# Fused attention and Fourier mixing: three copies of turned u on another engine, and some steps in another order

## The chip, the cores and the metric

The kernel runs on one core of a Trainium2 chip. The metric is the device time of the whole kernel in microseconds (us), the median of several runs. The engines are TensorE (PE, with its weight loads as PEld), VectorE (DVE), ScalarE (ACT) and GpSimd (POOL). SyncE (SP) does nothing but issue transfers (DMA); GpSimd and ScalarE issue a few as well.

## The reference

There are 8 batches of 8 heads, with 512 rows `x` and 32 rows `state` of 64 numbers for each head. Cut to what matters:

```
scores = scale * x @ state.T         # 512 x 32 for each head
xread  = softmax(scores)  @ state    # 512 rows
sread  = softmax(scale * state @ x.T) @ x   # 32 rows
x = concat(xread, sread)             # (8, 544, 512), heads side by side
u = x + real(fft(fft(x, axis=1), axis=2))
un = (u - mean(u)) / sqrt(var(u) + 1e-6)
out = u + relu(un @ w_ch1) @ w_ch2   # 512 -> 2048 -> 512
```

## The kernel before

The Fourier transforms are products with tables of sines and cosines. The 544 rows of a batch are folded onto each other, so that one product gives a row and its mirrored row. A batch passes through these stages:

- **Reading (`attend`).** The input rows lie in `xin` as bf16 with the rows on the partitions. For the scores they must be turned: `xT`, and `sT` for the state. Batches 0 and 1 turn on TensorE; from batch 2 on SyncE issues DMA transposes (L377 and L388, four for `xT`). `scores(i)` does 8 matmuls (L422) into one PSUM buffer, `esp`, and ScalarE takes the exponential into `E` (L427). The first call needs the first two of four row blocks, the second the other two. `turn_scores(g)` turns `E` by TensorE (L434), and ScalarE copies the result to `ET` (L435). The reads are then matmuls with `ET` (L447), divided by their sums on VectorE (L455, L456); the per head read of the state rows (`sread_by_head`, L467) ends in five VectorE operations (L470, L474). Folds on VectorE (L516 to L536) and GpSimd (L501 to L513) follow.
- **Mixing (`transform`).** `over_s` (L774) is the transform over rows, `over_d` (L670, L671) over columns. VectorE adds them to the reads, which gives four tiles `U[k, r]` of 128 rows. Each has its mean and variance taken on VectorE (L337, L339); GpSimd works out the root (L343, L344); and the centred tile `ub` is written by ScalarE (L814, L831) or VectorE (L812, L833). `turn_u(k, r)` turns it into a quarter of `unT`: on TensorE with a copy out of PSUM (L842, L843) in batches 0 and 1, by a DMA transpose (L838) from batch 2 on. In a later batch `centre(k, r)` does statistics and centring in one step.
- **The layers.** `layer1` has 16 steps (L917, or L927 in quarters for batch 0) that need `unT` and end in a Relu on ScalarE (L919, L929). `layer2` has four quarters for each of four tiles (L982), and the last quarter ends in `store`: VectorE scales and adds (L949), SyncE writes. Mirrored tiles go over `r_dram` (L963), and their second transfer (L964) is issued at the next store. The 32 state rows of a batch are kept for later in `XLs` by a ScalarE copy, `keep_middle` (L857), which `done1` calls for batch 1.

[...] the order of calls is the schedule. For batches 0 and 1 it is written out call by call (L1111 to L1244). There `L` and `M` are the steps of layer 1 and 2 of batch 0, `s1` and `r1` the scores and reads of batch 1, `turn_u` and `centre_sums` those of batch 0, and `turn_u1`, `centre1` and `done1` those of batch 1. In the loop at b = 1, `M1`, `L1`, `R`, `T` are layer 2 of batch 0 (from M[7] on), layer 1 of batch 1, the reads of batch 2 and the mixing of batch 2; `s2` and `s3` are the scores of batches 2 and 3. `T[7]` turns (0, 1) and centres (1, 1), `T[8]` turns (0, 0) and centres (1, 0), `M1[8]` is M[15], the last store of batch 0. From b = 2 on `weave` mixes the streams: each stream has a start and an end between 0 and 1, step i of n is put at start + (end − start)(i + 0.5)/n, and the steps are sorted. At b = 3 the reads are those of batch 4, and layer 2 is batch 2's.

PSUM is shared out in pools: `psQ` has three buffers that turned tiles, scores, turned scores and both transforms take in turn; `psF` has three for both layers; `psX` has one for the reads. A buffer is taken again once the last operation that reads it is done.

Of the kernel before, what the change touches and what calls it, by code (L numbers as in the profile page):

```python
# [30 lines left out]
def kernel(  # L31
# [8 lines left out]
    nc = tc.nc  # L40
# [71 lines left out]
    def load_state(lo, hi, src=state):  # L112
        nc.sync.dma_start(
            out=states(lo, hi).rearrange("p b g d -> p (b g) d"),
            in_=src[lo:hi].rearrange("b (g hh) j d -> (hh j) (b g) d", hh=4),
        )
# [4 lines left out]
    def load_x(b):  # L121
        xs = xs_of[b] if b in xs_of else wk.tile([128, 4 * dm], F32, name="xs", tag="xs")
        xs_of[b] = xs
        v = xs.rearrange("p (i h d) -> p i h d", i=4, d=D)
        xb = x[b].rearrange("h s d -> s h d")
        row = v[15:32:16, 3]
        parts = [
            (v[:, 0], xb[1:129]),
            (v[:, 1], xb[144:272]),
            (v[:, 2], xb[273:401]),  # L130
            (v[32:128, 3], xb[416:512]),
            (v[0:15, 3], xb[129:144]),
            (v[16:31, 3], xb[401:416]),
            (row, xb[0:273:272]),
        ]
        if b == 0:
            for queue, n in ((nc.sync, None), (nc.scalar, 2), (nc.sync, 3), (nc.scalar, 0), (nc.sync, 4), (nc.sync, 5), (nc.sync, 6),
                             (nc.sync, 1)):
                if n is None:
                    load_state(0, 1)  # L140
                else:
                    queue.dma_start(out=parts[n][0], in_=parts[n][1])
            return
        for o, rows in parts:
            nc.sync.dma_start(out=o, in_=rows)

    def cast_x(b, copy=nc.gpsimd.tensor_copy, lo=0, hi=4):
        copy(xin_bufs[b % 2][:, lo:hi, 1:513], xs_of[b].rearrange("p (i c) -> p i c", i=4)[:, lo:hi])  # L148
# [16 lines left out]
    def state_blocks(lo, hi, copy=nc.scalar.copy):  # L165
        for hh in range(4):
            pq = slice(32 * hh, 32 * hh + 32)
            copy(stb[pq, lo:hi, :, 4 + 64 * hh:68 + 64 * hh], states(lo, hi)[pq])
# [189 lines left out]
    turned = {}  # L358
# [546 lines left out]
    def layer1(key):  # L905
        low = isinstance(key, tuple)
        n = 128 if low else 512
        hT = wk.tile([128, FC, n], BF16, name="hTL" if low else "hT", tag="hTL" if low else "hT", bufs=1 if low else 2)
        h_of[key] = hT
        per = 512 // n  # L910

        def step(i):
            ph = psF.tile([128, 512], F32, name="ph", tag="c")
            for f in range(per * i, per * i + per):
                o = (f % per) * n
                for c in range(DC):
                    nc.tensor.matmul(ph[:, o:o + n], lhsT=w1[:, c, f * 128:(f + 1) * 128], rhs=un_of[key][:, c, :],  # L917
                                     start=(c == 0), stop=(c == DC - 1))
            nc.scalar.activation(hT[:, per * i:per * i + per, :].rearrange("p a b -> p (a b)"), ph, AF.Relu,  # L919
                                 scale=-1.0 / 512 if key == 0 else -1.0 if key in flipped else 1.0)  # L920

        def quarter_step(i, r):
            ph = psF.tile([128, 512], F32, name="ph", tag="c")
            for f in range(4 * i, 4 * i + 4):
                o = 128 * (f % 4)
                for c in range(DC):
                    nc.tensor.matmul(ph[:, o:o + 128], lhsT=w1[:, c, f * 128:(f + 1) * 128],  # L927
                                     rhs=un_of[key][:, c, 128 * r:128 * r + 128], start=(c == 0), stop=(c == DC - 1))
            nc.scalar.activation(hT[:, 4 * i:4 * i + 4, 128 * r:128 * r + 128], ph.rearrange("p (a b) -> p a b", b=128),  # L929
                                 AF.Relu, scale=-1.0 / 512 if key == 0 else -1.0 if key in flipped else 1.0)  # L930

        if key == 0:
            return [lambda i=i, r=r: quarter_step(i, r) for r in range(4) for i in range(FC // 4)]
        return [lambda i=i: step(i) for i in range(FC // per)]
# [55 lines left out]
    def weave(*streams):  # L990
        todo = []
        for n, (steps, lo, hi) in enumerate(streams):
            for i, s in enumerate(steps):
                if s is not None:
                    todo.append((lo + (hi - lo) * (i + 0.5) / len(steps), n, i, s))
        for _, _, _, s in sorted(todo, key=lambda t: t[:3]):
            s()
# [19 lines left out]
    begin, terms_of, low_of, out_of, keep_low, over_d, add_sums, centre_sums, turn_u, spread, done, keep_middle = transform(0)  # L1017
# [85 lines left out]
    s1, r1 = attend(1)  # L1103
    scores_next, reads_after = attend(2)
    L, M = layer1(0), layer2(0)
    over_s1, over_d1, add1, centre1, turn_u1, done1 = transform(1)
    turns1, copies1, s1 = s1[0], s1[1:4], s1[4:]
# [29 lines left out]
    L[1]()  # L1137
    turn_u(0, 0)
    s1[0]()
    s1[1]()  # L1140
    add_sums(1, 1)
    add_sums(1, 0)
    L[2]()
    L[3]()
    s1[2]()
    s1[3]()
# [10 lines left out]
    r1[4]()  # L1157
    r1[3]()
    centre_sums(1, 0)
    turn_u(1, 1)  # L1160
    L[7]()
    r1[5]()
    L[8]()
# [43 lines left out]
    centre1(1, 0)  # L1207
    done()
    first_roots[0]()
    M[3]()  # L1210
    spread(0, 0)
    first_roots[5]()
    M[7]()
    turn_u1(1, 1)
    M[8]()
    turn_u1(1, 0)
    done1()
    l2, scores_first = M, scores_next
    for b in range(1, B + 1):
        reads_next = reads_after  # L1220
        l2, l2_now = (layer2(b), [l2[7]] + l2[8:]) if b == 1 else (layer2(b) if b < B else [], l2)
        early, until, start = {2: (7, 0.25, 0.22), 3: (3, 0.13, 0.1)}.get(b, (0, 0, 0.08))
        l2_now = l2_now + (layer2(("L", b // 4)) if b in (3, 7) else [])
        streams = [(l2_now[:early], 0, until), (l2_now[early:], until + 0.02 if early else 0, 1)]
        if b == 1:
            M1, L1, R, T, s2 = l2_now, layer1(1), reads_next, transform(2), scores_first
            scores_next, reads_after = attend(3)
            s3 = scores_next
            def spreads():
                spread(1, 1)  # L1230
                spread(1, 0)
                for root in first_roots[6:8]:
                    root()

            def roots():
                for root in first_roots[1:5]:
                    root()

            for step in (spreads, M1[2], s2[0], s2[1], L1[0], M1[3], s2[2], s2[3], L1[1], lambda: cast_x(3), turned[3], L1[2],
                         lambda: load_state(4, B, s_dram), lambda: load_x(4), R[0], L1[3], R[1], roots, M1[4], R[2], L1[4], R[3], L1[5], R[4],  # L1240
                         L1[6], M1[5], R[6], L1[7], R[7], L1[8], M1[6], R[8], L1[9], L1[10], M1[7], T[0], T[1], L1[11], T[2], T[3],
                         L1[12], T[4], L1[13], s3[0], T[5], L1[14], s3[1], T[6], L1[15], T[7], M1[8], T[8], s3[2], s3[3], T[9], T[10],
                         T[11], lambda: state_blocks(4, B, nc.gpsimd.tensor_copy)):
                step()  # L1244
            continue
        if b < B:
            streams.append((layer1(b), start, 1))
        if b + 1 < B:
            reads, mix = {2: ((0.1, 0.45), (0.57, 0.88)), 3: ((0.03, 0.4), (0.5, 0.86))}.get(b, ((0, 0.375), (0.47, 0.85)))
            streams.append((reads_next, *reads))  # L1250
            streams.append((transform(b + 1), *mix))
        if b + 2 < B:
            scores_next, reads_after = attend(b + 2)
            streams.append(([lambda: (cast_x(b + 2), turned[b + 2]())], 0.2, 0.2))
            streams.append((scores_next, 0.5, 1))
        if b + 3 < B:
            streams.append(([lambda: load_x(b + 3)], 0.35, 0.35))
        if b in (3, 7):
            streams.append((low_rows(b // 4), 0.02, 0.2))
            streams.append((layer1(("L", b // 4)), 0.36, 0.8))  # L1260
        weave(*streams)
# [30 lines left out]
```

The softmax here doesn't subtract the row's maximum and nothing guards it: scores larger than these inputs give would overflow.

## Time and profile before

| what | value |
|---|---|
| time, median of 3 | 300.76 us (300.56 to 300.85) |
| span of the profiled run | 298.8 us |
| TensorE busy | 285.7 us, 96% |
| VectorE busy | 176.6 us, 59% |
| ScalarE busy | 139.5 us, 47% |
| GpSimd busy | 91.8 us, 31% |
| a matmul of 512 columns in either layer | 379 ns from start to end, 0.216 us from start to start |
| copy of turned u out of PSUM (L843) | 417 ns on VectorE (5 of them), 567 ns on ScalarE (3 of them) |

"Busy" is the time in which an engine has work, a share of the span. A row of the timeline gives a group's start and length in us, its engine, its line in the kernel, the operation with the tiles that it writes and reads, the shape, how many there are, and in brackets the engine's idle time before it with what ended that. Starts are counted from the first instruction. A few matmul records are missing, so a group of 3 may be one of 4.

### The profile page before, as it was taken

What the parts mean: (1) busy time and instruction counts of PE and PEld (TensorE: products, weight loads), DVE (VectorE), ACT (ScalarE), POOL (GpSimd) and SP (SyncE); (2) the same over time, 40 slices, a digit from 0 to 9 for tenths busy, and PEclk for the clock granted to TensorE, in tenths of its full rate; (3) what the DMA queues carried; (4) which work ended last, traced back from release to release, by engine and by line L of the source; (5) the groups of instructions that cost most, each with busy time, mean ns of one, the idle gap of its engine ahead of it and who ended that gap; (6) DMA issues with size and microseconds to landing.
All of it is one profiled execution on the core that took longest, in us unless ns stands there. A gap on an engine that the chain in (4) does not pass through costs nothing.

```text
span 298.8 us, 6004 instructions
## 1 busy us (share of the span) xinstructions
PE 285.7 (96%) x2288; PEld 163.3 (55%) x2319; DVE 176.6 (59%) x441; ACT 139.5 (47%) x260; POOL 91.8 (31%) x227
## 2 busy tenths in 40 slices
PE   5999899899899999999999999999999999999995
PEld 4689785445445544566444554455444544555443
DVE  8865789576769488645548394757567574111122
ACT  6888575545824662354523543344524443334200
POOL 6764833393590045202242033402240121000000
PEclk9999999999999999999999999999999999999999
DMA  9999993956965932684343955153332034400345
GB/s 157 189 203 198 149 169 63 172 140 144 192 132 101 225 69 58 136 161 119 81 105 80 187 104 142 38 116 78 99 96 43 30 89 98 113 24 16 98 117 135
DMA packets 110824, 34.86 MB, mean 117 GB/s; under 512 B 101980, under 2 KB 106332, under 8 KB 110796
## 3 DMA queue, kind: packets, MB, share of 16 engines
q1 hardware_dynamic: 100076, 28.72, 44.6%
q0 software_dynamic: 4224, 4.19, 9.7%
q10 hardware_dynamic: 6496, 1.57, 2.6%
q8 instruction: 18, 0.29, 0.5%
q14 instruction: 10, 0.08, 0.1%
HBM read 22.41 MB, written 14.02 MB: 122 GB/s over the span
## 4 chain that ended last, share of the span: by engine, by line
PE 82%; DVE 12%; ACT 2%; issue 2%; POOL 1%; DVEq 0%; POOLq 0%; ACTq 0%
PE po L982 33%; PE ph L917 32%; PE ph L927 5%; PE gp L774 3%; DVE st L337 2%; DVE U L675 2%; PE yp L670 1%; PE yp L671 1%; PE po L974 1%; DVE ot L949 1%; PE xrp L447 1%; PE eTp L434 1%; PE esp L422 1%; PE gp L717 1%; PE xfp L447 1%
## 5 line engine op out<-in xcount | busy, mean ns | idle before, releaser
L982 PE MATMUL po<-w,hT 128*128 128x512 bf16 x482 | 121.3, 379 | 1.2 <-issue 0.5
L919 ACT ACTIVATE hT<-ph 128x512 bf16<-128x512 f32 x112 | 66.9, 597 | 111.2 <-PE ph L917 109.7
L917 PE MATMUL ph<-unT,w 128*128 128x512 bf16 x431 | 111.8, 379 | 1.0 <-DVE ot L949 0.3
L917 PEld LDWEIGHTS <-w 128*128 128x128 bf16 x576 | 50.4, 98 | 46.1 <-issue 0.9
L982 PEld LDWEIGHTS <-hT 128*128 128x128 bf16 x496 | 46.8, 98 | 47.5
L949 DVE SCALAR_TENSOR_TENSOR ot<-po,rstd,U 128x512 f32<-128x512 f32 (+2 forms) x33 | 24.1, 731 | 51.7 <-PE po L982 46.0
L778 POOL COPY GL<-G 128x128 bf16<-128x128 bf16 x7 | 2.0, 291 | 68.3 <-ACT G L775 68.3
L337 DVE BATCH_NORM_STATS2 st<-U 128x6 f32<-128x512 f32 x32 | 21.8, 682 | 0.1
L344 POOL TENSOR_TENSOR rstd<-rstd,mhalf 128x1 f32<-128x1 f32 x34 | 20.8, 611 | 2.7
L343 POOL TENSOR_TENSOR rstd<-mv,epst 128x1 f32<-128x1 f32 x34 | 6.7, 198 | 47.2 <-DVE mv L339 47.2
L675 DVE TENSOR_TENSOR U<-yp,XR 128x512 f32<-128x512 f32 x14 | 9.5, 680 | 19.7 <-PE yp L671 19.7
L927 PE MATMUL ph<-unT,w 128*128 128x128 bf16 x256 | 15.6, 219 | 1.1 <-DVE unT L843 1.1
L927 PEld LDWEIGHTS <-w 128*128 128x128 bf16 x256 | 14.7, 98 | 1.5 <-DVE unT L843 1.1
L775 ACT CAST G<-gp 128x288 bf16<-128x288 f32 x28 | 12.9, 482 | 4.9 <-PE gp L774 4.9
L148 POOL CAST xin<-xs 128x2048 bf16<-128x2048 f32 (+1 forms) x9 | 11.7, 1319 | 2.6 <-DMA xs<-in_x_dram 2.5
L929 ACT ACTIVATE hT<-ph 128x512 bf16<-128x512 f32 x16 | 9.5, 599 | 5.7 <-PE ph L927 5.6
L455 DVE RECIPROCAL rs<-xrp 128x8 f32<-128x8 f32 x14 | 2.9, 206 | 14.2 <-PE xrp L447 14.2
L833 DVE TENSOR_SCALAR ub<-U,mv 128x512 bf16<-128x512 f32 x20 | 10.3, 514 | 0.7
L501 POOL COPY XT<-XR 32x514 bf16<-32x514 bf16 x7 | 4.2, 603 | 21.0 <-DVE XR L456 19.9
L456 DVE TENSOR_TENSOR XR<-xrp,rs 128x512 bf16<-128x512 f32 x14 | 9.7, 694 | 0.5
L456 DVE TENSOR_TENSOR XF<-xfp,rs 128x512 bf16<-128x512 f32 x14 | 9.7, 691 | 0.5
L427 ACT ACTIVATE E<-esp 128x512 bf16<-128x512 f32 x14 | 8.3, 596 | 3.1 <-PE esp L422 3.0
(240 smaller groups left out, 377.8 us busy)
## 6 DMA issues: line engine op xcount, KB each, us to landing
xs<-in_x_dram SPq DMA_DIRECT2D x22, 256.0 KB, 4.6
w<-in_moe_w_ch_dram POOLq DMA_DIRECT2D x8, 512.0 KB, 10.2
out_dram<-ot SPq DMA_DIRECT2D x15, 256.0 KB, 3.7
r_dram<-ot SPq DMA_DIRECT2D x14, 256.0 KB, 2.2
out_dram<-r_dram SPq DMA_DIRECT2D x14, 256.0 KB, 3.6
xs<-in_x_dram SPq DMA_DIRECT2D x8, 192.0 KB, 4.7
xs<-in_x_dram ACTq DMA_DIRECT2D x2, 256.0 KB
l_dram<-ot SPq DMA_DIRECT2D x2, 256.0 KB
```

Source lines behind the costliest of these rows:

```text
L148: copy(xin_bufs[b % 2][:, lo:hi, 1:513], xs_of[b].rearrange("p (i c) -> p i c", i=4)[:, lo:hi])
L337: nc.vector.bn_stats(st6, u)
L344: nc.gpsimd.tensor_tensor(rstd, rstd, mhalf, op=ALU.pow)
L456: nc.vector.tensor_tensor(ov, in0=p[ps, :, 0:256].rearrange("p g (h d) -> p g h d", d=D), in1=rs[ps].unsqueeze(3).to_broadcast([n, 2, 4, D ...
L675: nc.vector.tensor_add(u.rearrange("p (k r) -> p k r", r=2), p.rearrange("p (r k) -> p k r", r=2)[:, 0:u.shape[1] // 2, :], x.rearrange("p ...
L775: nc.scalar.copy(G[:, j, :].rearrange("p (i q) -> p q i", q=2), p[:, 0:NM].rearrange("p (q i) -> p q i", q=2))
L833: nc.vector.tensor_scalar(t, in0=ud, scalar1=mv[:, 0:1], scalar2=None, op0=ALU.subtract)
L917: nc.tensor.matmul(ph[:, o:o + n], lhsT=w1[:, c, f * 128:(f + 1) * 128], rhs=un_of[key][:, c, :], start=(c == 0), stop=(c == DC - 1))
L919: nc.scalar.activation(hT[:, per * i:per * i + per, :].rearrange("p a b -> p (a b)"), ph, AF.Relu, scale=-1.0 / 512 if key == 0 else -1.0 ...
L927: nc.tensor.matmul(ph[:, o:o + 128], lhsT=w1[:, c, f * 128:(f + 1) * 128], rhs=un_of[key][:, c, 128 * r:128 * r + 128], start=(c == 0), st ...
L949: nc.vector.scalar_tensor_tensor(ot[:, cols], in0=po_of[i][:, 0:cols.stop - cols.start], scalar=rstd, in1=u[:, cols], op0=ALU.mult, op1=AL ...
L982: nc.tensor.matmul(po_of[i], lhsT=h_of[key][:, f, i * 128:(i + 1) * 128], rhs=w2[:, f, :], start=(f == 0), stop=(f == FC - 1))
```

## The change

The change touches the order and one choice of engine; no computation is added or taken away.

- Three copies of turned u, batch 0's (1, 1) and batch 1's (1, 1) and (1, 0), go from VectorE to ScalarE. VectorE's queue is then clear of them.
- The second scores of batch 1 (`s1[1]`) come after the step `L[2]` and batch 0's additions rather than right after the first scores, so that they don't wait for a buffer of `psQ`.
- `M[3]`, which ends in a store, comes after the statistics of batch 0's (0, 0) and its root.
- `done1` moves from before the loop to behind the turned scores of batch 2.
- In the loop at b = 1, `T[7]` and `T[8]`, which centre batch 2's tiles on ScalarE, move behind the turned scores of batch 3 (`s3[2]`, `s3[3]`); `M1[8]` is then ahead of both.
- At b = 3 the reads begin at 0.04 instead of 0.03. By the rule of `weave` this changes one place: the per head read of batch 4 goes from 0.174 to 0.18, behind layer 2's store at 0.175.

```diff
     s1[0]()
-    s1[1]()
     add_sums(1, 1)
     add_sums(1, 0)
     L[2]()
+    s1[1]()
     L[3]()
...
     centre_sums(1, 0)
-    turn_u(1, 1)
+    turn_u(1, 1, nc.scalar.copy)
     L[7]()
...
     first_roots[0]()
-    M[3]()
     spread(0, 0)
     first_roots[5]()
+    M[3]()
     M[7]()
-    turn_u1(1, 1)
+    turn_u1(1, 1, nc.scalar.copy)
     M[8]()
-    turn_u1(1, 0)
-    done1()
+    turn_u1(1, 0, nc.scalar.copy)
...
-            for step in (spreads, M1[2], s2[0], s2[1], L1[0], M1[3], s2[2], s2[3], L1[1], lambda: cast_x(3), turned[3], L1[2],
+            for step in (spreads, M1[2], s2[0], s2[1], L1[0], M1[3], s2[2], s2[3], done1, L1[1], lambda: cast_x(3), turned[3], L1[2],
...
-                         L1[12], T[4], L1[13], s3[0], T[5], L1[14], s3[1], T[6], L1[15], T[7], M1[8], T[8], s3[2], s3[3], T[9], T[10],
+                         L1[12], T[4], L1[13], s3[0], T[5], L1[14], s3[1], T[6], L1[15], M1[8], s3[2], s3[3], T[7], T[8], T[9], T[10],
...
-            reads, mix = {2: ((0.1, 0.45), (0.57, 0.88)), 3: ((0.03, 0.4), (0.5, 0.86))}.get(b, ((0, 0.375), (0.47, 0.85)))
+            reads, mix = {2: ((0.1, 0.45), (0.57, 0.88)), 3: ((0.04, 0.4), (0.5, 0.86))}.get(b, ((0, 0.375), (0.47, 0.85)))
```

## The prediction

> **What bounds the kernel now.** I read the page's busy line first, then the waits of TensorE, then TensorE's timeline for where they lie, then the same microseconds on ScalarE, GpSimd and SyncE.
>
> ```profile
> PE 285.7 (96%) x2288; PEld 163.3 (55%) x2319; DVE 176.6 (59%) x441; ACT 139.5 (47%) x260; POOL 91.8 (31%) x227
> ```
>
> TensorE is busy for 96% of the span, and the change takes no matmul away. All it can win is TensorE's idle time. In the timeline the bracket is the idle time before a group and what ended it:
>
> ```profile
> 24.95 0.39 PE L422 MATMUL esp<-sT,xT 128*128 128x64 bf16 x8 [0.21 <-DVE unT L843]
> 33.38 1.07 PE L927 MATMUL ph<-unT,w 128*128 128x128 bf16 x16 [0.78 <-DVE unT L843]
> ...
> 54.17 0.39 PE L422 MATMUL esp<-sT,xT 128*128 128x64 bf16 x8 [0.84 <-DVE unT L843]
> ...
> 78.25 2.75 PE L982 MATMUL po<-w,hT 128*128 128x512 bf16 x12
> 81.80 0.28 PE L447 MATMUL xrp<-stb,ET 128*128 128x260 bf16 x1 [0.79 <-ACT ET L435]
> 82.37 0.28 PE L447 MATMUL xrp<-stb,ET 128*128 128x260 bf16 x1 [0.29 <-ACT ET L435]
> ...
> 86.62 1.04 PE L917 MATMUL ph<-unT,w 128*128 128x512 bf16 x3
> ...
> 119.66 1.02 PE L917 MATMUL ph<-unT,w 128*128 128x512 bf16 x4 [0.29 <-DVE ot L949]
> ```
>
> The bracket is a little short of the loss: a run of 12 matmuls takes 2.75 us at 0.379 each, so they start every (2.75 − 0.379)/11 = 0.216 us, and without a wait the next would start 0.16 us before the shown end. With 0.16 added, the six stalls cost 0.37, 0.94, 1.00, 0.95, 0.45 and 0.45: 4.2 us. After 120 us TensorE runs without a stall. The change aims at exactly these six, so the question is what each removal runs into. There, transfers matter:
>
> ```profile
> 0.00:46.00 46.00, 40.33 (x618) 34.82 (x620) 34.27 (x124) 34.09 (x64) 28.53 (x92) 1.00 1.09 173
> 46.00:54.00 8.00, 7.28 (x52) 4.00 (x52) 6.75 (x16) 4.76 (x8) 2.42 (x9) 1.00 0.37 77
> ```
>
> The last two numbers are the DMA share and GB/s. Up to 46 us the 16 DMA engines are full (share 1.09), so what lands about then doesn't come earlier because TensorE is quicker. GpSimd's and SyncE's timelines show what hangs on it:
>
> ```profile
> 45.17 1.27 POOL L168 CAST stb<-gen 32x128 bf16<-32x128 f32 x4 [0.81 <-DMA gen<-s_dram]
> 46.50 0.19 POOL L1171 CAST gate<-w 128x4 f32<-128x4 bf16 x1
> 46.63 0.21 POOL L1109 CAST xin<-xs 128x16 bf16<-128x16 f32 x1
> ```
> ```profile
> 46.87 5.12 SPq L388 DMA_TRANSPOSE xT<-xin  x4
> 52.03 5.29 SPq L145 DMA_DIRECT2D xs<-in_x_dram  x7
> ...
> 77.74 0.38 SPq L953 DMA_DIRECT2D out_dram<-ot  x1
> 78.26 1.66 SPq L838 DMA_TRANSPOSE unT<-ub  x1
> 80.02 0.52 SPq L963 DMA_DIRECT2D r_dram<-ot  x1
> 81.06 3.84 SPq L838 DMA_TRANSPOSE unT<-ub  x3
> ```
> ```profile
> xT<-xin SPq DMA_TRANSPOSE x24, 2.5
> unT<-ub SPq DMA_TRANSPOSE x24, 2.3
> ```
>
> GpSimd waits for a transfer until 45.17, finishes batch 2's input at 46.84, and SyncE issues the four transposes of x, the last about 46.87 + 5.12 − 1.26 = 50.7. They land 2.5 us after issue: the last at 53.2. The second scores of batch 2, at 54.17, read it. So there the margin is 0.95 us, no more. And the last transpose of u of batch 2 is issued at 81.06 + 3.84 − 1.22 = 83.7 and lands at about 86.0; layer 1 of batch 2 starts at 86.62. Margin 0.6.
>
> [...] 567 ns for ScalarE's copy of turned u (L843), and 417 ns for VectorE's. [...] VectorE's copy at 53.71 stands behind the eviction L949 that waited 0.94 us for GpSimd's root. [...]
>
> **Opening (scores of batch 1 apart).** The second scores wait until turn_u(0, 0)'s PSUM buffer is copied out; with L[2] (16 matmuls of 0.055, 0.89 us) between, the copy is long done: −0.37. In return the second exponential stands behind L[2]'s Relu on ScalarE. That Relu starts 1.10 us after L[2] does (26.27 against 25.17), so now at 24.51 + 1.10 = 25.61; the exponential follows at 26.1, ends at 26.7, and TensorE wants it for turning at 26.96 − 0.4 = 26.5. 0.2 is given back: net −0.2.
>
> **turn_u(1, 1) of batch 0 by ScalarE.** VectorE's copy waits behind a centring of 0.92 us and a read; ScalarE is idle then (1.20 us before its Relu at 32.33). The turns end at 31.4, 0.57 us of copy at 32.0, and L[8] is reached at 32.44: the 0.94 goes. VectorE is rid of 0.41 us there. What queues behind the copy on ScalarE is L[7]'s Relu, whose matmuls end at 32.3.
>
> **Batch 1's last two turns by ScalarE, M[3] behind the spread.** The second scores of batch 2 need the buffer of turn_u1(1, 1). ScalarE centres (1, 0) until 51.44 and then is nearly free until 53.37, so two copies of 0.57 fit and the buffers are out of the way; moving M[3] only lets GpSimd's root for M[7] start earlier, and both evictions have until 56 us. The 1.00 goes. But TensorE now reaches these scores at 53.18 − 0.2 − 0.94 = 52.0, and the transposed x lands at 53.2. It waits until about 53.3. **So by here 54.17 − 53.3 = 0.87 us is won, not 2.1.**
>
> **done1 later.** It moves a ScalarE copy of 0.61 us between the turned scores and L1[1]'s Relu. That Relu (57.82 to 58.42) frees the buffer that L1[3] takes at 58.65; a margin of 0.23. ScalarE starts such operations every 0.5 us, so the Relu ends at 58.9: a new wait of 0.3. Won so far: 0.57.
>
> **Centrings behind turned scores.** ScalarE's ET copies (81.07, 81.64) stood behind a centring that waited for VectorE until 80.44. Now they follow the turning at 78.3 and are done by 79.9 on the old scale; the reads want them at 80.84. 0.95 + 0.45 goes. Layer 1 of batch 2 is then reached at 86.62 − 0.57 − 1.40 = 84.65. Its unT, however, comes from SyncE, which was issuing without a break from 62 to 78 us, started by the transposes at 46.87, so it can't be earlier. Now M[15]'s store goes first (its eviction ends at about 78.3 on the new scale; 0.52), then four transposes from 79.0: at 1.3 each, the first perhaps 1.66 again, the last is issued between 83.1 and 83.7 (the latter if the pause before 81.06 stays) and lands 2.3 to 2.5 later. ub(1, 0) is ready at about 80.8 and isn't what binds. TensorE starts between 85.6 and 86.1 rather than at 86.62: **0.5 to 1.0 won by here, I take 0.75.** The wait of 0.3 above and the opening's 0.2 vanish in this one.
>
> **Per head read behind a store.** With the start 0.04, only the fourth read step of batch 4 changes places, at 0.18 behind the store at 0.175. The store's eviction (118.85, 0.75 us) no longer waits for the five VectorE operations (1.5 us) of that read; it ends near 118.1, and L1[2] wants its buffer at 119.2. −0.45, and the read's rows have until the fold at 123.
>
> **Sum.** 0.75 + 0.45 = 1.2: 300.76 − 1.2 = 299.6 us.
>
> **Rivals.** (1) All six stalls vanish: 300.76 − 4.2 = 296.6. For it: the brackets name VectorE and ScalarE alone. Against: the landings at 53.2 and 86. (2) The transposes of u go out without the pauses and don't bind: 0.57 + 1.40 + 0.45 = 2.4, so 298.4. For it: the pause before 81.06 has no named cause. (3) They land at about 86.3 to 86.6 as before, since they now queue behind a store: 0 to 0.3 + 0.45 is won, 300.3. (4) Slower: the four transposes each behave like the first (1.66 to issue, 3.6 to land, as the one at 78.26 did): last issue 79.0 + 3 × 1.7 = 84.1, landing 87.7, TensorE 1.1 later than before, less 0.45: 301.4. For it: the transfers of x land in the same stretch. Against: the three that followed took 1.3.
>
> **Chances.** The forecast 0.60; (1) 0.04, (2) 0.14, (3) 0.13, (4) 0.09. The range takes in (2) and (3), 298.3 to 300.4. Faster by over 0.2% (under 300.16): the forecast, (1), (2), and a part of (3): 0.82. Same 0.09, slower 0.09.
>
> **What would show it.** TensorE's waits after should have no VectorE unT of batch 0 or 1 and no ET. They should have scores L422 of batch 2 waiting about 1.2 us for the DMA of xT, L917 waiting about 0.3 us for a Relu some 5 us later, and about 1 us for the DMA of unT near 85.5. If TensorE is at layer 1 of batch 2 without a wait, I am wrong by the transposes; if that start is later than 86.6, the store in front of them cost more than I gave it.

## The result, and the profile after

The changed kernel takes 298.44 us (median of 4, 297.88 to 298.91) against 300.7 for the kernel before on the same chip (4 runs, 300.56 to 300.85): a ratio of 0.9924 [0.9902, 0.9946]. It is 2.3 us faster. Ratios rest on fast runs: one slower run below (303.79 us, at a granted clock of 0.994) is not in them. The forecast was 299.6 with a range from 298.3 to 300.4, so the direction held, the result lies just inside the lower end of the range, and the forecast was 1.2 us too cautious. The rival at 298.4 hit the number; whether for its reason is the question below.

The page's line of busy times after the change:

```profile
PE 287.1 (97%) x2319; PEld 163.6 (55%) x2319; DVE 175.6 (59%) x438; ACT 140.7 (48%) x263; POOL 91.6 (31%) x227
```

TensorE's timeline after the change, at the places of the six stalls:

```profile
24.56 1.06 PE L927 MATMUL ph<-unT,w 128*128 128x128 bf16 x16
25.46 0.40 PE L422 MATMUL esp<-sT,xT 128*128 128x64 bf16 x8
...
51.73 0.63 PE L422 MATMUL esp<-sT,xT 128*128 128x64 bf16 x16
52.19 1.03 PE L917 MATMUL ph<-unT,w 128*128 128x512 bf16 x4
...
56.94 1.02 PE L917 MATMUL ph<-unT,w 128*128 128x512 bf16 x4 [0.43 <-ACT hT L919]
...
79.12 0.39 PE L447 MATMUL xrp<-stb,ET 128*128 128x260 bf16 x2
...
83.11 0.43 PE L467 MATMUL srp<-xin,E 128*32 128x64 bf16 x32
84.39 1.02 PE L917 MATMUL ph<-unT,w 128*128 128x512 bf16 x4 [0.85 <-DMA unT<-ub]
...
116.96 1.03 PE L917 MATMUL ph<-unT,w 128*128 128x512 bf16 x4
117.82 1.03 PE L982 MATMUL po<-w,hT 128*128 128x512 bf16 x4
```

All six old brackets are gone. Two new ones stand: layer 1 waits for a Relu (L919) at 56.94, and for the transposed u of batch 2 at 84.39. Nothing waits at 51.73, where the scores of batch 2 read the transposed x; the forecast had put its largest new wait there.

The balance closes when the same step is followed through both timelines. The layer 1 step behind the second scores of batch 2 starts at 54.50 before and at 52.19 after: 2.31 us won, as much as the first three stalls together (0.37 + 0.94 + 1.00). (This is the step `L1[0]` of the loop.) The turned scores of batch 3 start at 77.78 before and 76.06 after: 1.72, so the Relu's wait gave back 0.59. Layer 1 of batch 2 starts at 86.62 and 84.39: 2.23, that is 1.72 plus 1.43 from the two ET stalls, less 0.92 for u. From there to the end of the span it takes 212.20 before and 211.71 after: 0.49 more, the last stall. Together 2.7, the difference of the two spans (298.8 and 296.1).

Where the missing wait at 51.73 went is told by SyncE's and GpSimd's timelines of the changed kernel:

```profile
45.16 5.12 SPq L388 DMA_TRANSPOSE xT<-xin  x4
...
76.24 0.38 SPq L953 DMA_DIRECT2D out_dram<-ot  x1
77.05 0.34 SPq L963 DMA_DIRECT2D r_dram<-ot  x1
77.51 5.65 SPq L838 DMA_TRANSPOSE unT<-ub  x4
```
```profile
43.47 1.26 POOL L168 CAST stb<-gen 32x128 bf16<-32x128 f32 x4 [0.33 <-DMA gen<-s_dram]
44.79 0.19 POOL L1171 CAST gate<-w 128x4 f32<-128x4 bf16 x1
44.92 0.21 POOL L1109 CAST xin<-xs 128x16 bf16<-128x16 f32 x1
```

GpSimd has `gen` at 43.47 rather than 45.17, and the transposes of x begin at 45.16 rather than 46.87. The forecast had taken that start as fixed. Much of what SyncE does up to 84 us follows from it, but not all: SyncE has issued the store at 76.24 by 76.62 and begins the next one, `M[15]`'s (L963), only at 77.05, right after that tile's eviction on VectorE (76.28 + 0.74 = 77.02):

```profile
76.28 0.74 DVE L949 SCALAR_TENSOR_TENSOR ot<-po,rstd,U 128x512 f32<-128x512 f32 x1
```

The four transposes of u stand behind that store in SyncE's queue: the first of them is issued at 77.51, though its u was written by 74.96 (L831 on ScalarE, 74.24 + 0.72). So two things can set when they start: the chain of transfers that SyncE issues from the first transpose of x on ("the chain" from here on), or TensorE's own progress, through `M[15]`'s eviction. The experiments ask whether this chain of transfers sets the gain (theory A in the expectations) or whether the removed stalls simply add up (theory B), and whether the chain's start moves with the change or by itself.

### The profile page after: what moved, and what is told of

The parts are those of the page before. It is cut to its first block, busy times and chain, and to the rows that moved or that the text cites. A ratio compares the mean times of both kernels' runs of the same rounds, so it can differ in the third digit from the quotient of the medians.

```text
span 296.1 us, 6036 instructions
## 1 busy us (share of the span) xinstructions
PE 287.1 (97%) x2319; PEld 163.6 (55%) x2319; DVE 175.6 (59%) x438; ACT 140.7 (48%) x263; POOL 91.6 (31%) x227
## 4 chain that ended last, share of the span: by engine, by line
PE 89%; DVE 3%; ACT 3%; issue 1%; DMA 1%; SPq 1%; POOL 0%; DVEq 0%; POOLq 0%
PE po L982 36%; PE ph L917 34%; PE ph L927 5%; PE gp L774 3%; PE yp L670 1%; PE yp L671 1%; PE po L974 1%; PE xfp L447 1%; PE eTp L434 1%; PE esp L422 1%; PE xrp L447 1%; ACT ub L831 1%; DMA unT<-ub 1%; PE gp L717 1%; PE gp L751 1%
## 5 line engine op out<-in xcount | busy, mean ns | idle before, releaser
L982 PE MATMUL po<-w,hT 128*128 128x512 bf16 x496 | 123.4, 379 | 0.0
L919 ACT ACTIVATE hT<-ph 128x512 bf16<-128x512 f32 x112 | 66.7, 597 | 110.9 <-PE ph L917 110.5
L917 PE MATMUL ph<-unT,w 128*128 128x512 bf16 x448 | 113.7, 379 | 1.3 <-DMA unT<-ub 0.9
L675 DVE TENSOR_TENSOR U<-yp,XF 128x510 f32<-128x510 f32 x14 | 9.4, 673 | 0.0
```

The costliest lines, as they stand in the source:

```text
L675: nc.vector.tensor_add(u.rearrange("p (k r) -> p k r", r=2), p.rearrange("p (r k) -> p k r", r=2)[:, 0:u.shape[1] // 2, :], x.rearrange("p ...
L982: nc.tensor.matmul(po_of[i], lhsT=h_of[key][:, f, i * 128:(i + 1) * 128], rhs=w2[:, f, :], start=(f == 0), stop=(f == FC - 1))
```

## The experiments

Every ratio below is against the kernel before, run on the same chip in the same rounds.

**The changed kernel once more.** No edit.

> The changed kernel once more, to see how far its profiled stage moves from one execution to the next. Theory A (a chain of transfers bounds it: the issues of SyncE begin with batch 2's transposes of x at 45.2 us, run without a break, and end in the transposes of u of batch 2, for which layer 1 waits at 84.4): the time follows the start of that chain, which moves by some tenths of a us between executions, so times spread over 0.5 us or more, about 298.0 to 299.0, and the profile shows layer 1 of batch 2 starting 39.2 us after the first transpose. Theory B (the removed waits simply add up, 2.3 us, and no transfer bounds): times within 0.3 us as before the change, and the start of layer 1 of batch 2 keeps its distance from the opening instead.

299.14 us (6 runs, 298.78 to 299.81), 0.9941 [0.9924, 0.9958]. The profiled execution began the transposes of x at 46.33 and layer 1 of batch 2 at 85.29; from there to the end it took 211.71 again. A's distance of 39.2 us is met (38.96), but the chain's start is not what made this execution longer. Its waits:

```profile
PE ph L927 <- DMA w<-in_moe_w_ch_dram: 0.9, 1, 0.9
PE ph L917 <- DMA unT<-ub: 0.8, 1, 0.8
```

The first of them is a wait of 0.85 for the last quarter of w1 at 26.71, long before the chain. It makes TensorE late: `L1[0]` starts at 53.12 instead of 52.19, and layer 1 of batch 2 follows 32.17 us later, as it did in the first profile (32.20). `M[15]`'s store again waits for its eviction (SyncE is free at 77.68, the eviction ends and the store begins at 77.96 to 77.98).

**done1 where it was.**

```diff
     turn_u1(1, 0, nc.scalar.copy)
+    done1()
...
-... s2[2], s2[3], done1, L1[1] ...
+... s2[2], s2[3], L1[1] ...
```

> done1 goes back to before the loop. The stall of 0.43 us (0.6 with the start-up) of L917 on a Relu near 57 us should vanish in both theories. Theory A: the wait for the turned u of batch 2 grows by the same 0.6, and the time is that of the changed kernel within 0.2 us. Theory B: 0.6 us less than the changed kernel.

299.45 (9 runs, 298.72 to 300.74), 0.9955 [0.9937, 0.9973]. The waits of TensorE in its profile (us in total, times, longest):

```profile
PE ph L917 <- DMA unT<-ub: 1.2, 1, 1.2
...
PE esp L422 <- DMA xT<-xin: 0.2, 1, 0.2
```

The wait for the Relu is gone, as the forecast's reasoning on `done1` has it, and nothing is won, where B asked for 0.6 us. Part of the 0.59 comes back as waits for transfers: 0.23 for x, and 1.17 for u instead of 0.82 to 0.98 in the three profiles of the unedited kernel. SyncE comes to `M[15]`'s store without a pause here (77.53, the store at 77.66, the eviction over by 77.44), so in this execution the chain binds. That is A.

**The two centrings where they were.**

```diff
-... L1[15], M1[8], s3[2], s3[3], T[7], T[8], T[9], T[10],
+... L1[15], T[7], M1[8], T[8], s3[2], s3[3], T[9], T[10],
```

> The two centring steps of batch 2 go back ahead of the turned scores of batch 3. The reads wait again for ET, 0.8 and 0.3 us (1.4 with the start-ups). Theory A: the wait of 0.85 us (1.0) for the turned u of batch 2 takes most of that in, so the loss is 0.4 us or less against the changed kernel, unless the transposes, no longer behind a store, come earlier too. Theory B: 1.4 us slower than the changed kernel.

299.18 to 299.63 in four of the five runs (303.79 in the fifth), 0.9949 [0.993, 0.9967]; 299.62 in the profiled execution. Its waits:

```profile
PE xrp L447 <- ACT ET L435: 1.1, 2, 0.8
PE esp L422 <- DMA xT<-xin: 0.7, 1, 0.7
PE ph L917 <- ACT hT L919: 0.4, 1, 0.4
```

Both ET stalls are back in full (0.79 and 0.29 in the brackets), and the wait for u is gone in exchange; layer 1 of batch 2 starts at 86.09. B asked for 1.4 us; between this ratio and that of the unedited changed kernel lie 0.0008, some 0.2 us, which their intervals don't resolve, though they do exclude 1.4. One transpose of u is ahead of `M[15]`'s store again by this edit; even so the last one is issued 29.59 us after `L1[0]`, beside 29.73 to 29.88 in the unedited kernel. This execution also shows the wait that the forecast expected, 0.70 us for the transposed x; its chain began at 46.74.

**The opening as before**: the second scores of batch 1 at once, `turn_u(1, 1)` copied by VectorE.

```diff
     s1[0]()
+    s1[1]()
...
     L[2]()
-    s1[1]()
...
-    turn_u(1, 1, nc.scalar.copy)
+    turn_u(1, 1)
```

> The second scores of batch 1 directly after the first, and batch 0's turn_u(1, 1) on VectorE again. Its two waits return, about 0.4 and 0.9 us. Theory A: the waits later on, for turned u of batch 2 above all, shrink by what is lost here, so that at most 0.3 us is lost against the changed kernel. Theory B: 1.2 us slower than the changed kernel.

299.42 (5 runs, 299.34 to 299.81), 0.9951 [0.9934, 0.9967]. Waits:

```profile
PE ph L917 <- DMA unT<-ub: 1.4, 1, 1.4
PE ph L927 <- DVE unT L843: 1.1, 2, 0.8
PE ph L917 <- ACT hT L919: 0.4, 1, 0.4
```

The stall of 0.78 is back, and yet TensorE reaches layer 1 of batch 2 early enough to wait 1.40 us there; SyncE comes to the store without a pause (78.43, the store at 78.56). The edit adds stalls of 1.3 us and costs about 0.3 by the medians of the same rounds, so B's 1.2 is not met. The profiled execution alone would not show this: at 299.81 it is 1.0 to 1.9 us longer than the three of the unedited kernel. Its chain began at 46.86, later than in any of them.

**A transfer out of the way.** The copy of a result tile from its scratch to the output (L964 of `M[3]`'s tile), which makes SyncE idle for 2.8 us in front of it, goes to a later store.

```diff
-            while later:
+            while later and (key, i) != (0, 1):
```

> The changed kernel, but the second transfer of batch 0's first mirrored tile (L964) is issued at M[11]'s store instead of M[7]'s. Theory A (SyncE's chain bounds): SyncE stands idle for 2.8 us before it, from 57.0 to 59.8, since it waits for the first transfer to land; without that the chain up to the transposes of u of batch 2 is 2 to 3 us shorter, the wait of L917 for the turned u (0.85, 1.0 with the start-up) vanishes, and the time falls by 1.0 us against the changed kernel. Theory B (no chain bounds, the removed waits add up): no change within 0.2 us.

298.45 (11 runs, 297.89 to 300.63), 0.9937 [0.9917, 0.9957]. The expected gain of 1.0 didn't come: the wait for u stays at 0.93.

**The same, with done1 behind `L1[3]`** (`L1[3], done1, R[1]`).

> The same, and done1 behind L1[3], where ScalarE is idle. Theory A: with the chain out of the way the stall of 0.6 us on a Relu is no longer swallowed by a later wait, so its removal now pays in full: 1.6 us less than the changed kernel, while it paid nothing when done1 alone was moved. The times should also lie closer together, within 0.3 us, as nothing depends on when the transfers land. Theory B: 0.6 us less than the changed kernel.

298.57 (6 runs, 297.29 to 299.1), 0.9918 [0.9898, 0.9937]; the expected gain of 1.6 didn't come either, and the wait for u is 0.87. SyncE's timeline of this run shows why neither edit shortens it:

```profile
74.01 0.65 SPq L964 DMA_DIRECT2D out_dram<-r_dram  x1
74.77 1.14 SPq L953 DMA_DIRECT2D out_dram<-ot  x1
78.10 0.35 SPq L963 DMA_DIRECT2D r_dram<-ot  x1
78.58 5.65 SPq L838 DMA_TRANSPOSE unT<-ub  x4
```

SyncE is through with everything else at 75.91 and then idles for 2.2 us. The next in its queue is `M[15]`'s store (L963), which waits for that tile's eviction, and behind it stand the four transposes, the first of which is issued at 78.58 (its u was written by about 76.0 in the profile of the edit before this one, 75.3 + 0.72). So with SyncE free earlier, this store binds, and through its eviction TensorE's own progress; in the profile after the change it already held SyncE from 76.62 to 77.05.

**The chain's start moved on purpose.** GpSimd no longer reads from w2's last quarter ahead of batch 2's input, and casts that input before the states. The removed line only orders transfers; nothing of the computation is left out.

```diff
-    state_blocks(3, 4, nc.gpsimd.tensor_copy)
-    nc.gpsimd.tensor_copy(gate, w2[:, 12:16, 0])
...
     turned[2]()
+    state_blocks(3, 4, nc.gpsimd.tensor_copy)
```

> The changed kernel with batch 2's last input columns no longer cast after the second layer's last weights have landed and after batch 3's state, so that the transposes of x of batch 2 are issued at about 43.3 us, some 2 to 3 us earlier, beside the last weights. Theory A: the chain begins earlier, the wait for the turned u of batch 2 goes (1.0 us) unless the transposes are held up by the weights' transfer as much as they were moved. Theory B: the same time as the changed kernel within 0.2 us.

298.07 (6 runs, 297.92 to 299.13), 0.9915 [0.99, 0.9929]. The transposes of x begin at 43.41, 1.8 us before the earliest of the changed kernel. Layer 1 of batch 2 starts at 84.43 all the same: SyncE stands from 75.38 to 77.14 at `M[15]`'s store, and the wait for u is 0.81. An early chain alone runs into that store: against the first profile of the changed kernel the chain began 1.75 us earlier, and layer 1 of batch 2 0.04 later.

**The kernel before, profiled anew**, twice, to see how far its own chain moves.

> The kernel before once more. If the start of the chain (first transpose of x of batch 2: 46.87 before, 45.16 and 46.33 in two profiles of the changed kernel) moves with the execution, this profile shows another value than 46.87 by some tenths, and the time stays within 0.3 us of before in any case, since there the last transpose of x leaves 0.95 us. If the change itself had brought the transfers forward, 46.9 comes again.

> The kernel before a third time, for the start of the chain alone (first transpose of x of batch 2: 46.87 and 48.09 in its two profiles, 45.16, 46.33 and 45.58 in three of the changed kernel). If only the execution moves it, a value down to 45.2 can come here too; if the change moves it as well, 46.5 or more comes again.

Times 300.69 (12 runs, 300.56 to 301.51), 1.0002 [0.9993, 1.0011], and 301.71 in the one run of the other. Chains began at 48.09 and 48.62, after 46.87 in the first profile. In both, layer 1 of batch 0 also waits for the last quarter of w1, near 27 us (0.76 and 0.86), which the first profile doesn't show; the changed kernel has it in some executions too (0.85 in its second profile).

**Two transposes of u ahead of that store.** In batch 2, `T[7]` and `T[8]` are split: u is sent to be transposed before `M1[8]`, the centrings stay behind the turned scores. On top of the two edits on the transfer and `done1`.

```diff
-... L1[15], M1[8], s3[2], s3[3], T[7], T[8], T[9] ...
+... L1[15], T[7], T[8], M1[8], s3[2], s3[3], T[9] ...
```
(here `T[7]` and `T[8]` are `turn_u(0, 1)` and `turn_u(0, 0)`; `centre(1, 1)` and `centre(1, 0)` follow as the new `T[9]` and `T[10]`)

> transfer_and_done1, and the first two transposes of u of batch 2 (their tiles were centred before) issued ahead of M[15]'s store. Theory A as it stands after the last runs (the chain or, once it is shorter, M[15]'s eviction in front of all four transposes: SyncE stood idle from 75.9 to 78.1 for it): the last transpose is issued some 1.5 us earlier, near 81, the wait of 0.87 us (1.0) of L917 for the turned u goes, and the time is 1.0 us below transfer_and_done1 and 1.6 below the changed kernel in executions in which the opening's transfers land alike. Theory B (the wait that transfer_and_done1 kept came from something else than the order of store and transposes): no change within 0.2 us.

297.93 (6 runs, 297.0 to 299.61), 0.9907 [0.9886, 0.9928]; the unedited kernel in the same rounds (the last experiment below) has 298.99. That is 1.1 us less, where 1.6 was expected. The wait for u, which `transfer_and_done1` had kept (0.87), is gone from the profiled execution:

```profile
82.98 0.43 PE L467 MATMUL srp<-xin,E 128*32 128x64 bf16 x32
83.47 1.02 PE L917 MATMUL ph<-unT,w 128*128 128x512 bf16 x4
```

Its chain began at 45.63 and `L1[0]` at 52.54, as in the profile of the unedited kernel beside it (45.58 and 52.54), and the last transpose of u was issued at 81.05 instead of 82.42. This shows what the wait for u hangs on: four transposes in a row behind `M[15]`'s store.

**The same, with the chain's start moved.**

> turns_first, and batch 2's x turned without waiting for the last weights and for batch 3's state (as no_gate). Theory A: nothing of SyncE's chain is left to bind and scores of batch 2 no longer wait for their x either, which some executions of transfer_later and opening kernels showed with 0.2 to 0.85 us; the time is that of turns_first or up to 0.8 us less, and the times lie within 0.5 us of each other. Theory B: as transfer_and_done1.

296.68 (4 runs, 296.52 to 297.24), 0.9867 [0.9852, 0.9881]. This version beats both kernels, and is 1.25 us below the one before it (0.8 at most was expected). Its SyncE timeline, and TensorE's:

```profile
71.49 1.36 SPq L953 DMA_DIRECT2D out_dram<-ot  x1
74.44 2.83 SPq L838 DMA_TRANSPOSE unT<-ub  x2
77.80 0.36 SPq L963 DMA_DIRECT2D r_dram<-ot  x1
78.27 2.55 SPq L838 DMA_TRANSPOSE unT<-ub  x2
```
```profile
82.57 0.43 PE L467 MATMUL srp<-xin,E 128*32 128x64 bf16 x32
82.92 1.04 PE L917 MATMUL ph<-unT,w 128*128 128x512 bf16 x4
```

The store still holds SyncE (to 77.80), but only two transposes stand behind it, and layer 1 follows the reads without a bracket. Taken together: removing the six stalls is worth 4.1 of the 4.2 us that the brackets held by the medians (3.9 by the spans of the first profile and this one), once the Relu's wait and the two on transfers are gone too. The changed kernel itself took some 1.7 to 2.3 of it.

**The changed kernel beside these two.**

> The changed kernel on the same chip as the two above, to compare with. Theory A: 298.4 to 299.2 us, layer 1 of batch 2 begins 211.7 us before the end, and it waits there for the turned u by about 1 us. Theory B: the same time, but without that wait.

298.99 (10 runs, 297.98 to 301.3), 0.9945 [0.9924, 0.9965]; chain from 45.58, layer 1 of batch 2 at 84.88. A's wait for u is there in this execution (0.98 in the bracket), and the 211.7 us to the end as well.

All the profiled executions of the changed kernel and its derivatives in which layer 1 of batch 2 waits for u, and the one with the centrings back, can be laid side by side (us). "Pause" is how long SyncE stands before `M[15]`'s store; without a wait about 0.1 passes there.

| execution | first transpose of x | `L1[0]` | layer 1 of batch 2 | behind the transpose | behind `L1[0]` | pause | its time |
|---|---|---|---|---|---|---|---|
| chain's start moved on purpose | 43.41 | 52.27 | 84.43 | 41.02 | 32.16 | 1.75 | 297.95 |
| changed, first | 45.16 | 52.19 | 84.39 | 39.23 | 32.20 | 0.44 | 297.88 |
| changed, beside the last two | 45.58 | 52.54 | 84.88 | 39.30 | 32.33 | 0.13 | 298.37 |
| done1 back | 46.18 | 52.81 | 85.13 | 38.95 | 32.32 | 0.13 | 298.72 |
| changed, once more | 46.33 | 53.12 | 85.29 | 38.96 | 32.17 | 0.30 | 298.78 |
| transfer later | 46.57 | 53.22 | 85.49 | 38.92 | 32.27 | 0.54 | 298.97 |
| transfer later, done1 behind L1[3] | 46.67 | 53.31 | 85.46 | 38.79 | 32.16 | 2.19 | 298.96 |
| centrings back | 46.74 | 53.37 | 86.09 | 39.35 | 32.71 | 0.11 | 299.62 |
| opening back | 46.86 | 53.55 | 86.30 | 39.44 | 32.75 | 0.13 | 299.81 |

Without the first row, the distance behind the first transpose of x stays within 0.65 us, which looks like A. But the distance behind `L1[0]` stays within 0.59, so these rows alone cannot tell the two apart. The first row and the pauses can. Where SyncE pauses for the eviction (0.30 us and more), layer 1 of batch 2 lies 32.16 to 32.27 behind `L1[0]`, over chain starts from 43.41 to 46.67: there TensorE's own progress sets it. Where SyncE comes to the store without a pause and the wait for u follows, the chain sets it. Of the three profiles of the changed kernel two are of the first kind, one of the second, and in all three the two lie within 0.4 us of each other. So the changed kernel stands between two bounds that nearly tie, and neither A nor B holds as it was put: moving the chain alone won nothing against the first profile, removing a stall of TensorE alone (`done1`) won nothing, and taking two transposes from behind the store did.

The chain's start does act on TensorE itself: late chains made it wait for x (0.23 to 0.85 us in three of these executions), and that moves `L1[0]`. The wait for w1 moves it as well (0.85 and 1.02 in two), so the longer executions of the changed kernel are not all the chain's doing.

Not every part of the change was undone alone: batch 1's two turns, `M[3]` and the per head read were not. For these the positions in the profiles before and after are the only evidence.

## Why the forecast was too cautious, step by step

- **Opening, −0.2.** The stall of 0.37 went; the second exponential gave back 0.1 (turning waits at 26.80) rather than the 0.2 worked out. Right in kind. The first three stalls still come out at 2.31: gaps too short for a bracket, such as 0.2 us near 51.0 before, are gone after and make up for it.
- **turn_u(1, 1) of batch 0, and batch 1's two turns.** Both stalls went, costed at 0.94 and 1.00. That ScalarE had room is right.
- **"It waits until about 53.3 … 0.87 us is won, not 2.1."** This is the term that was mis-sized: it measured 2.31. The mechanism was right, since the wait appeared in executions where the chain began late (0.70 with a start at 46.74, 0.85 with 46.57; not with 46.67, where TensorE had already lost 1.02 to w1), but the forecast took the start of SyncE's transposes from one profile, 46.87, as a constant of the kernel. In the changed kernel it was 45.16, 46.33 and 45.58.
- **done1, "a new wait of 0.3".** It measured 0.59. The copy costs 0.62 of ScalarE's time and small gaps around it, so the Relu begins 0.78 later on the old scale, not the 0.5 taken from the distance of ScalarE's starts.
- **Centrings, −1.40.** 1.43.
- **"TensorE starts between 85.6 and 86.1 … 0.5 to 1.0 won by here, I take 0.75."** It measured 2.23, from the same term: TensorE comes earlier by what it did not wait for x, so `M[15]`'s eviction is over at 77.02 instead of the 78.3 of the forecast, and SyncE is free earlier too. From the store on the forecast was right: u is what binds, the pause stayed, and the last transpose is issued 4.9 us after the eviction (4.8 to 5.4 in the forecast).
- **Per head read behind a store, −0.45.** 0.46 to 0.49: the stretch from layer 1 of batch 2 to the end is 212.20, 212.17 and 212.18 in three profiles of the kernel before and 211.71 in all three of the changed one.

The rival at 298.4 had u not binding and the transposes without pauses. That isn't what happened: u binds (0.92 us), and the pause in front of the second transpose of u is still there. That its number was met is luck: x came earlier than the rival assumed, by more than u took back. The rival with a store in front of the transposes saw the right object but not its use: `M[15]`'s store doesn't undo the gain, it keeps an earlier chain from being worth more. The rival at 296.6 describes the version that reached 296.68, not the change.

**What stays open** is whether the change itself brings the chain forward. The eight profiles with the opening's part and GpSimd's old order began it between 45.16 and 46.74, on average at 46.1. The four without that part (three of the kernel before, and the opening put back) began it between 46.86 and 48.62, on average at 47.6. In the same eight the transfer of `gen` is issued at 36.97 to 39.16, in the four at 39.18 to 40.88. That points to the opening, which brings TensorE forward by 1.2 us well before that issue. But the two sets nearly touch, the changed kernel alone spreads over 1.2 us, and a profile with GpSimd's order changed and the opening in it issued `gen` at 39.86. In the first profiles before and after the change SyncE waits 6.7 and 5.0 us for a transfer into `s_dram` to land, and then issues `gen`. In the twelve that transfer is issued between 28.18 and 29.83; from the one issue to the other it takes 8.5 to 10.5 us in the eight and 10.3 to 11.1 in the four, so these overlap too. The kernel before with the opening's part alone wasn't run. So the link from the opening to the chain's start is argued, not shown. What is shown is that x landed early enough in the profile after the change, and that `M[15]`'s store with four transposes behind it makes layer 1 of batch 2 wait.

## What to carry to other kernels

When TensorE's stalls are removed in front of a step that reads a transferred tile, look for the first instruction of the queue that issues the transfer and ask what sets its start; where that hangs on transfers that ran while the DMA engines were full (here at a share of 1.09, where the start of the transposes of x lay anywhere from 46.87 to 48.62 in three profiles of one program), take it as a range over several executions, not from one profile. A queue that issues transfers one after another can be a bound like any engine (four transposes of u took SyncE 5.65 us), and so can a store in it that waits for an engine (it held SyncE for up to 2.19 us): shortening one only uncovered the other here (the wait for u stayed at 0.81 to 0.93 us), so move what others wait for ahead of the stores that nobody waits for. Undone edits that each cost far less than the stall they bring back are a sign of such a bound. And when two starts move together over many executions, look for an execution that moves one alone before calling it the cause.

## What the runs showed of the hardware

- The DMA engines' share up to 46 us is 1.09 in the first profile of the kernel before and 1.04 in that of the changed one. What hangs on a transfer there moved by 1.76 us between executions of one program: GpSimd had `gen` at 45.17, 46.33 and 46.93 in three of the kernel before. Most of that is its issue, at 39.25, 40.17 and 40.88, which waited for an earlier transfer (6.7 us in the first of the three); from issue to use it took 5.9 to 6.2 in each. Yet 34 of the 39 times of that kernel beside the last two sets of runs lie between 300.56 and 300.97. After the change the spread of the times grew (297.98 to 301.3 over 10 runs). Profiles show waits of up to 0.85 us for w1 or x in the longer executions; that these make up the whole spread isn't shown.
- Issuing takes time of its own: SyncE spends 1.19 to 1.27 us on issuing a transpose of u in the changed kernel, half of the 2.4 us (median) in which it lands, and layer 1 of batch 2 waited 0.85 us for the last of four such issues in a row (5.65 us).
- One of the four transposes of u comes late: 1.75 to 1.78 us after the one before it, where the others follow at 1.30 to 1.38. It is the second in the three profiles of the changed kernel and with the opening back, and the third in both runs with the transfer later. In the first profile of the changed kernel SyncE shows one semaphore instruction of 17 ns in the 0.5 us before it and nothing else, and the u it reads had been ready since 76.54, 2.7 us before its issue at 79.28. The cause wasn't found.
